# A convolution and a gated two-layer product on one core: a cast and a load moved in the opening, two PSUM banks and the last store changed at the end

## The chip, the cores and the metric

The kernel runs on one core of one Trainium2 chip. The metric is the device time of one execution in microseconds; the median of three runs is used. Five engines run their own queues in program order and wait for each other by semaphores: TensorE (PE, with its weight loads as PEld), VectorE (DVE), ScalarE (ACT), GpSimd (POOL) and SyncE (SP, which here issues nearly all DMAs). Matrix products land in PSUM[...].

## What is computed

```python
# x: (8, 4096, 192), weight: (8 heads, 7), w_in: (192, 2048), w_out: (2048, 192), all float32
w = softmax(weight, axis=-1)
# causal convolution over the sequence, each head of 24 channels with its own 7 weights
y[b, s, head] = sum_k w[head, k] * x[b, s - 6 + k, head]       # zeros ahead of the sequence
h = y.reshape(32768, 192) @ w_in
g = h * cos(h)
out = g @ w_out                                                # (32768, 192)
```

## The kernel before, in words

The 32768 tokens are cut into 32 units of 1024 and 64 tiles of 512. A unit is loaded (`load_unit`, L66), cast to bfloat16 with its channels reordered (`cast_unit`, L157: three copies, L170 for the even heads, L171 and L172 for the odd heads with the partition halves exchanged), convolved on PE with banded matrices (`conv_mm`, L177), copied out of PSUM (`conv_out`, L186), doubled on POOL (`double_unit`, L236) and transposed by a DMA (`turn_unit`, L240). A tile is then eight steps `h0` to `h7`: six matmuls each (`mm1`, L316) into one slot of a ring of three PSUM tiles of two banks (`h_pool`), the sine with a shift on ACT (L330), and the product on DVE (L334), which frees the slot. The product with w_out (`mm2_step`, L340) sums into two further banks, `o_ps0` and `o_ps1` (L347). It uses the upper and the lower 64 rows of the array at once, for different sums, so that two matmuls run side by side; since both row halves of a sum go to one bank, an SP instruction (`Turn`, L141) stands between the end of one half and the start of the other. `evac` (L359) copies a bank to SBUF on ACT, and `store` (L364) writes a tile of 384 KB.

The order on each engine is written out by hand: strings give PE's and ACT's order in a tile (L371 to L375), and the rest of the loop (L377 to L425) says where copies, transposes, loads and stores come in. Two extra rounds of that loop drain the pipeline: round 64 has only `mm2` work (the last tile's sums begin, those of the tile ahead end), round 65 only the last 32 matmuls, those of the last sum's second row half.

The opening, L61 to L310, is a chain of its own. SP loads unit 0 in halves, w_in in four parts and unit 1. PE computes matmuls on zeros (`keep_warm`, L93) while DVE makes the banded weights: a product of 2128 columns (L253) and four sums (L256) give `prod`, and eight small copies, dealt out to DVE, ACT and POOL (L259 to L264), put it into `band`; three casts of w_in follow (L266). The first half of unit 0 is cast by ACT, the second half by POOL, both ahead of the bands in program order (L249 and L250). PE convolves the first half (two groups of eight matmuls), the second (two groups), and then transposes the first half itself (`turn_first`, L282); ACT and DVE copy each group out. The second half goes through `double_unit` and `turn_unit` (L301 and L302), after which SP issues the four loads of w_out (L303 to L305), POOL casts the second half of w_in (L306), unit 1 (L307) and w_out in two halves (L308 and L309), and unit 2 is loaded (L310). The first tile runs with the convolution of unit 1 among its steps (L374).

Of the kernel before, what the change touches and what calls it, by code (L numbers as in the profile page):

```python
# [8 lines left out]
FP32 = mybir.dt.float32  # L9
# [7 lines left out]
def kernel(  # L17
# [8 lines left out]
    nc = tc.nc  # L26
# [5 lines left out]
    T = 512  # L32
    NT = NTOK // T
    NB = T // 128
    U = 1024
    NU = NTOK // U
    UB = U // 128
# [18 lines left out]
    o_pools = [ctx.enter_context(tc.tile_pool(name=n, bufs=1, space=PSUM)) for n in ("o_p", "o_q")]  # L56
# [20 lines left out]
    HP = NP // 2  # L77
    for q in range(2):
        for t in range(2):
            nc.sync.dma_start(out=w_f[64 * t : 64 * t + 64, :, q * HP : (q + 1) * HP, :].rearrange("p k j f -> p k (j f)"),  # L80
                              in_=w_src[t, :, :, q * HP * 128 : (q + 1) * HP * 128])
    load_unit(1)
    wo_f = consts.tile([128, NP, 2, D], FP32)
    wo_src = moe_w_out.rearrange("(i j p) d -> p j i d", i=2, p=128)


    one = consts.tile([128, 128], FP32)
    nc.vector.memset(one, 1.0)
# [4 lines left out]
    def keep_warm(n):  # L93
        for _ in range(n):
            nc.tensor.matmul(out=idle, lhsT=zero[:, 0:128], rhs=zero, start=True, stop=True)  # L95
# [4 lines left out]
    w_all = o_pools[1].tile([128, T], FP32, name="o_ps1")  # L100
    w_bc = w_all[:, 0 : H * K].rearrange("p (h k) -> p h k", k=K)
    nc.tensor.matmul(out=w_all[:, 0 : H * K], lhsT=one[0:1, :], rhs=w_row, start=True, stop=True)
    keep_warm(16)


    xb0 = xbf_pool.tile([128, UB + 1, D], BF16, name="x_bf")
# [50 lines left out]
    def cast_unit(u, n0=0, n1=UB):  # L157
        copy = nc.scalar.copy if u == 0 and n0 == 0 else nc.gpsimd.tensor_copy
        if u == 0:
            bf[u] = xb0  # L160
        else:
            bf[u] = xbf_pool.tile([128, UB + 1, D], BF16, name="x_bf")
            if u % UPS == 0:
                nc.gpsimd.memset(bf[u][:, 0, :], 0.0)
            else:
                nc.gpsimd.tensor_copy(out=bf[u][:, 0, :], in_=bf[u - 1][:, UB, :])  # L166

        o = bf[u][:, n0 + 1 : n1 + 1, :].rearrange("p n (h t k r) -> t p (n h) k r", t=2, k=NC, r=R)
        i = x_tiles[u][:, n0:n1, :].rearrange("p n (h t r k) -> t p (n h) k r", t=2, k=NC, r=R)
        copy(out=o[0], in_=i[0])  # L170
        copy(out=o[1, 0:64], in_=i[1, 64:128])  # L171
        copy(out=o[1, 64:128], in_=i[1, 0:64])  # L172
        bf.pop(u - 2, None)
# [23 lines left out]
    def ring_banks():  # L197
        h = h_pool.tile([128, 2, T], FP32, name="h")
        return [h[:, 0, :], h[:, 1, :]]
# [36 lines left out]
    def double_unit(u, n0=0, n1=UB):  # L236
        ct = ct_tiles[u]
        nc.gpsimd.tensor_copy(out=ct[:, n0:n1, :, 1, :], in_=ct[:, n0:n1, :, 0, :])  # L238

    def turn_unit(u, n0=0, n1=UB):  # L240
        ct = ct_tiles.pop(u)
        if u not in cT:
            cT[u] = cT_pool.tile([128, UB, NC, 128], BF16, name="cT")
        nc.sync.dma_start_transpose(out=cT[u][:, n0:n1].rearrange("p n c k -> p (n c) k"),
                                    in_=ct[:, n0:n1].rearrange("p n c t k -> p (n c t k)"))
        cT.pop(u - 2, None)


    cast_unit(0, 0, NB)  # L249
    cast_unit(0, NB, UB)  # L250

    prod = consts.tile([128, K, H, E], BF16)
    nc.vector.tensor_tensor(out=prod, in0=mask.rearrange("p k (o e) -> p k o e", o=1).to_broadcast([128, K, H, E]),  # L253
# [6 lines left out]
    for odd in range(2):  # L260
        for q in range(4):
            e0 = 32 * (q ^ (2 * odd))
            three[(4 * odd + q) % 3](out=band[32 * q : 32 * q + 32, odd:H:2, e0 : e0 + E],  # L263
                                     in_=prod[32 * q : 32 * q + 32, 0, odd:H:2, :])  # L264
    for k in range(NC):
        three[(k + 2) % 3](out=w[:, k, 0:HP], in_=w_f[:, k, 0:HP])  # L266

# [4 lines left out]
    def conv_first(n0, n1):  # L272
        for c in range(2):
            ps = ring_banks()
            for i in range(4):
                for prev in range(2):
                    conv_mm(0, c, ps, i, slice(0, 128), prev, n0, n1, start=prev == 0 and i % 2 == 0, stop=prev == 1)
            yield
            for half in range(2):
                conv_out(0, c, ps, n0, n0 + 2 * half, n0 + 2 * half + 2, copies[half], double=n0 == 0)  # L280
# [12 lines left out]
    b = conv_first(NB, UB)  # L293
# [6 lines left out]
        list(across[half])  # L300
    double_unit(0, NB, UB)  # L301
    turn_unit(0, NB, UB)  # L302
    for q in range(2):  # L303
        for i in range(2):
            nc.sync.dma_start(out=wo_f[:, q * HP : (q + 1) * HP, i], in_=wo_src[:, q * HP : (q + 1) * HP, i])  # L305
    nc.gpsimd.tensor_copy(out=w[:, :, HP:NP], in_=w_f[:, :, HP:NP])  # L306
    cast_unit(1)  # L307
    for q in range(2):  # L308
# [19 lines left out]
    def gcu(t, j, h):  # L328
        cs = cos_pool.tile([128, 2, T], BF16, name="cs")
        nc.scalar.activation(out=cs, in_=h, func=AF.Sin, bias=math.pi / 2.0, scale=1.0)  # L330
        if j == 0:
            g_tiles[t] = gpool.tile([128, NF, T], BF16, name="g")
            g_tiles.pop(t - 3, None)
        nc.vector.tensor_tensor(out=g_tiles[t][:, 2 * j : 2 * j + 2, :], in0=h, in1=cs, op=ALU.mult)  # L334
# [5 lines left out]
    def mm2_step(t, q):  # L340
        half, i = divmod(q, STEPS)
        f, si = divmod(i, 2)
        for r, (tt, b) in enumerate(((t - 1, half), (t - 1, 0) if half else (t - 2, 1))):
            if not 0 <= tt < NT:
                continue
            if r == 0 and i == 0:
                o_ps[tt, b] = o_pools[b].tile([128, T], FP32, name="o_ps%d" % b)  # L347
            rows = slice(64 * r, 64 * r + 64)
            s = 2 * b + si
            m = nc.tensor.matmul(out=o_ps[tt, b][:, si * D : (si + 1) * D],  # L350
                                 lhsT=g_tiles[tt][rows, f, s * 128 : (s + 1) * 128], rhs=wo[rows, f // 2, f % 2, :],
                                 start=(r == 0 and i == 0), stop=(r == 1 and i == STEPS - 1), skip_group_check=True)
            if r == 0 and i == STEPS - 1:
                turns[tt, b] = Turn()
                turns[tt, b].mark(m)
            if r == 1 and i == 0:
                turns.pop((tt, b)).wait(m)

    def evac(t, b):  # L359
        if b == 0:  # L360
            o_sb[t] = opool.tile([128, NB, D], FP32, name="o_sb")
        nc.scalar.copy(o_sb[t][:, 2 * b : 2 * b + 2, :].rearrange("p s d -> p (s d)"), o_ps.pop((t, b))[:, 0 : 2 * D])  # L362

    def store(t):  # L364
        nc.sync.dma_start(out=out[t * T : (t + 1) * T, :].rearrange("(n p) d -> p n d", p=128), in_=o_sb.pop(t))

    o_ps, o_sb, turns = {}, {}, {}

# [8 lines left out]
    for t in range(NT + 2):  # L377
        u, second = divmod(t, TPU)
        cu, cc = (u + 2, 0) if second else (u + 1, 1)
        conv = {"c": conv_part(cu, cc, ring_banks if t else o_banks) if cu < NU else iter(())}  # L380
        if t == 0:
            conv["d"] = conv_part(1, 0, o_banks)
        act, done, h, step = (ACT_ORDER if t > 1 else ACT_FIRST[t]).split(), set(), {}, 0

        def flush():
            while act:
                k = act[0]
                need = {"P": "start", "Q": "|", "e": k[1:] + "2"}.get(k[0], "h" + k[1:])
                if need not in done:
                    return  # L390
                act.pop(0)
                if k == "P" and 0 <= t - 2 < NT:
                    evac(t - 2, 0)
                elif k == "Q" and 0 <= t - 2 < NT:
                    evac(t - 2, 1)
                elif k[0] == "e":
                    next(conv[k[1]], None)
                elif k[0] == "s" and t < NT:
                    gcu(t, int(k[1:]), h.pop(int(k[1:])))

        done.add("start")
        flush()
        for k in (PE_ORDER if t > 1 else PE_FIRST[t]).split():
            if k[0] == "h" and t < NT:
                h[int(k[1:])] = mm1(t, int(k[1:]))
            elif k[0] in conv:
                next(conv[k[0]], None)
            elif k[0] == "m":
                for q in range(step, step + int(k[1:])):
                    mm2_step(t, q)  # L410
                step += int(k[1:])
            done.add(k)
            flush()

            if k == ("|" if t == 0 else "h1") and second == 0 and cu < NU:
                double_unit(cu)
            if k == "|":
                if second == 0 and cu < NU:
                    turn_unit(cu)
                if 0 <= t - 2 < NT:  # L420
                    store(t - 2)
                if second == 1 and u + 3 < NU:
                    load_unit(u + 3)
                if second == 0 and u + 2 < NU:
                    cast_unit(u + 2)  # L425
# [30 lines left out]
```

## Time and profile before

The time is 737.81 us, the median of three runs from 736.77 to 737.82. The profiled execution has a span of 736.2 us.

| | |
|---|---|
| one tile, at 100 to 111 us, all engines | 11.04 us; PE busy 11.04, DVE 9.52, ACT 9.67, POOL 2.62 |
| warm-keeping matmuls, first to last | 1.33 to 7.81 us |
| first matmul of the convolution | 10.85 us |
| first matmul of the first tile | 16.37 us |
| granted PE clock from 11.97 to 15.38 us | 0.50 of full |
| last matmul ends, last copy by ACT | 732.1 us, 732.15 to 732.63 us |
| w_out loads issued; landed | 17.4 to 19.1 us; 4.1, 4.7, 6.1 and 8.1 us later |
| last store issued; landed | 732.68 us; 2.5 us later |

In the lines of the timeline the first number is the start, the second the time from the start of the first to the end of the last instruction of the row, then the engine, the source line, the operation, what it writes and reads, how many instructions, and in brackets how long the engine had been idle and what ended that. "PEld" is a weight load, "SPq" an instruction of SP's queue. In the page's second part each digit is the busy tenth of a fortieth of the span.

### The profile page before, as it was taken

The page shows a single profiled execution, that of the slowest core. Times are in us where ns is not written, and L with a number is a line of the kernel's source. Part 1 is how long each engine was busy: PE and PEld are TensorE (multiplying, and loading weights), DVE is VectorE, ACT ScalarE, POOL GpSimd, SP SyncE. Part 2 cuts the span into 40 slices and gives each one's busy share as a digit, 9 for nine tenths or more (in the row PEclk, how much of TensorE's full clock was granted, in tenths as well). Part 3 has the DMA queues.
Part 4 walks back from the last instruction along what each step waited for, and adds up shares of the span by engine and source line. Part 5 has one row for each costly group of instructions (what it writes and reads, how often), then busy time and mean ns, then how long its engine had stood idle before and what let it go on. Part 6 is the DMA issues. An engine that isn't in the chain of part 4 may idle for free.

```text
span 736.2 us, 26768 instructions
## 1 busy us (share of the span) xinstructions
PE 720.7 (98%) x12073; PEld 554.7 (75%) x12073; DVE 621.1 (84%) x538; ACT 626.8 (85%) x785; POOL 179.2 (24%) x177
## 2 busy tenths in 40 slices
PE   6799999999999999999999999999999999999997
PEld 3577777777777777777777777777777777777776
DVE  6888888888888888888888888888888888888883
ACT  5888888888888888888888888888888888888883
POOL 6522211222211222211222211222211222211000
PEclk9999999999999999999999999999999999999999
DMA  7734334344345454334344334344335455333301
GB/s 190 199 86 131 86 111 129 87 111 130 81 116 131 86 111 130 88 110 130 87 110 130 89 110 130 87 110 130 89 108 132 87 110 125 94 108 87 89 23 66
DMA packets 167941, 79.97 MB, mean 109 GB/s; under 512 B 99475, under 2 KB 167059, under 8 KB 167827
## 3 DMA queue, kind: packets, MB, share of 16 engines
q1 hardware_dynamic: 167824, 78.26, 40.3%
q8 instruction: 94, 1.54, 0.9%
q14 instruction: 21, 0.16, 0.1%
q10 hardware_dynamic: 2, 0.00, 0.0%
HBM read 28.31 MB, written 25.17 MB: 73 GB/s over the span
## 4 chain that ended last, share of the span: by engine, by line
PE 95%; ACT 0%; issue 0%; SPq 0%
PE o_ps L350 46%; PE h L324 45%; PE h L180 4%; ACT o_sb L362 0%; SPq L146 0%
## 5 line engine op out<-in xcount | busy, mean ns | idle before, releaser
L334 DVE TENSOR_TENSOR g<-h,cs 128x1024 bf16<-128x1024 f32 x512 | 609.1, 1221 | 98.4 <-ACT cs L330 89.8
L330 ACT ACTIVATE cs<-h 128x1024 bf16<-128x1024 f32 x512 | 511.5, 1025 | 79.7 <-PE h L324 78.4
L350 PEld LDWEIGHTS <-g 64*128 64x128 bf16 x8192 | 362.2, 94 | 68.1 <-SPq L146 1.8
L350 PE MATMUL o_ps<-wo,g 64*128 64x192 bf16 x8192 | 409.1, 243 | 1.8 <-ACT o_sb L362 1.2
L324 PE MATMUL h<-cT,w 64*128 64x512 bf16 x3072 | 401.4, 376 | 2.6 <-DVE g L334 1.4
L324 PEld LDWEIGHTS <-w 64*128 64x128 bf16 x3072 | 166.4, 94 | 85.3 <-issue 3.6
L238 POOL COPY ct<-ct 128x1536 bf16<-128x1536 bf16 (+1 forms) x32 | 46.2, 1444 | 492.5 <-issue 489.3
L362 ACT COPY o_sb<-o_ps 128x384 f32<-128x384 f32 x128 | 61.3, 479 | 11.0 <-PE o_ps L350 8.2
L195 ACT CAST ct<-h 128x384 bf16<-128x384 f32 (+1 forms) x124 | 52.4, 474 | 9.8 <-PE h L180 5.9
L180 PE MATMUL h<-x_bf,band 64*128 64x192 bf16 (+1 forms) x752 | 54.3, 243 | 5.1 <-DVE band L263 3.0
L180 PEld LDWEIGHTS <-band 64*128 64x128 bf16 (+1 forms) x776 | 38.7, 95 | 18.9 <-POOL band L263 3.9
L170 POOL CAST x_bf<-x_f 128x768 bf16<-128x768 f32 (+1 forms) x32 | 40.4, 1262 | 2.0 <-DMA x_f<-in_x_dram 2.0
L171 POOL CAST x_bf<-x_f 64x768 bf16<-64x768 f32 (+1 forms) x32 | 38.9, 1216 | 2.0
L172 POOL CAST x_bf<-x_f 64x768 bf16<-64x768 f32 (+1 forms) x32 | 38.5, 1204 | 1.9
L166 POOL COPY x_bf<-x_bf 128x192 bf16<-128x192 bf16 x24 | 8.2, 343 | 0.0
L95 PE MATMUL o_ps<-zero 128*128 128x512 bf16 x19 | 6.0, 473 | 1.3 <-DVE zero L90 1.3
L95 PEld LDWEIGHTS <-zero 128*128 128x128 bf16 x19 | 2.0, 114 | 4.0 <-issue 1.4
L309 POOL CAST wo<-wo_f 128x1536 bf16<-128x1536 f32 x2 | 2.9, 1466 | 4.7 <-DMA wo_f<-in_moe_w_out_dram 4.7
L263 ACT COPY band<-prod 32x152 bf16<-32x152 bf16 x3 | 0.9, 316 | 2.6 <-DVE prod L256 2.6
L256 DVE TENSOR_TENSOR prod<-prod 128x304 bf16<-128x304 bf16 (+1 forms) x4 | 2.7, 705 | 0.1
L253 DVE TENSOR_TENSOR prod<-mask,wn 128x2128 bf16<-128x2128 bf16 x1 | 2.4, 2376 | 0.1
L180 PE MATMUL o_ps<-x_bf,band 64*128 64x192 bf16 x24 | 2.0, 242 | 0.5 <-ACT ct L195 0.3
(43 smaller groups left out, 28.0 us busy)
## 6 DMA issues: line engine op xcount, KB each, us to landing
out_dram<-o_sb SPq DMA_DIRECT2D x64, 384.0 KB, 2.9
x_f<-in_x_dram SPq DMA_DIRECT2D x31, 768.0 KB, 5.2
w_f<-in_moe_w_in_dram SPq DMA_DIRECT2D x4, 384.0 KB, 8.1
wo_f<-in_moe_w_out_dram SPq DMA_DIRECT2D x4, 384.0 KB, 5.4
x_f<-in_x_dram SPq DMA_DIRECT2D x2, 384.0 KB, 4.0
cT<-ct SPq DMA_TRANSPOSE x32, 4.6
w_row<-in_weight_dram ACTq DMA_DIRECT2D x1, 0.2 KB
```

Source lines behind the costliest of these rows:

```text
L166: nc.gpsimd.tensor_copy(out=bf[u][:, 0, :], in_=bf[u - 1][:, UB, :])
L170: copy(out=o[0], in_=i[0])
L171: copy(out=o[1, 0:64], in_=i[1, 64:128])
L172: copy(out=o[1, 64:128], in_=i[1, 0:64])
L180: return nc.tensor.matmul(out=ps[i // 2][:, 0 : (n1 - n0) * 2 * G].rearrange("p (n k i r) -> p i n k r", n=n1 - n0, k=NC, i=2)[:, i % 2], ...
L195: copy(o[:, :, 0, :], i[:, :, 0, :])
L238: nc.gpsimd.tensor_copy(out=ct[:, n0:n1, :, 1, :], in_=ct[:, n0:n1, :, 0, :])
L324: nc.tensor.matmul(out=h[:, i, :], lhsT=w[rows, k, j, :], rhs=c[rows, n0 : n0 + NB, k, :], start=(k == 0), stop=(k == NC - 1))
L330: nc.scalar.activation(out=cs, in_=h, func=AF.Sin, bias=math.pi / 2.0, scale=1.0)
L334: nc.vector.tensor_tensor(out=g_tiles[t][:, 2 * j : 2 * j + 2, :], in0=h, in1=cs, op=ALU.mult)
L350: m = nc.tensor.matmul(out=o_ps[tt, b][:, si * D : (si + 1) * D], lhsT=g_tiles[tt][rows, f, s * 128 : (s + 1) * 128], rhs=wo[rows, f // 2, ...
L362: nc.scalar.copy(o_sb[t][:, 2 * b : 2 * b + 2, :].rearrange("p s d -> p (s d)"), o_ps.pop((t, b))[:, 0 : 2 * D])
```

## The change

Four edits. In the opening, the second half of unit 0 is cast by POOL after the eight band copies instead of ahead of them, and PE computes 26 matmuls on zeros instead of 16 while it waits, so that POOL leaves DVE alone while the bands are made. Half of w_out is loaded right behind unit 1, ahead of the transpose of unit 0's second half, so that it is there when POOL comes to cast it. At the end, the last tile's two sums go into the two banks of a slot of the ring, which is free by then, instead of `o_ps0` and `o_ps1`, so that they need not wait for the evacuation of the tile ahead; and the last tile is stored in two halves, each when its bank has been copied. The changed kernel's lines are 4 to 11 higher than those of before: the sums are L261, the band copies L268, the cast L176 to L178, the w_in casts L272, `mm1` L328, the sine L334, the product L338, `mm2` L358, `evac` L370, `store` L373.

```diff
+    def load_wo(q):
+        for i in range(2):
+            nc.sync.dma_start(out=wo_f[:, q * HP : (q + 1) * HP, i], in_=wo_src[:, q * HP : (q + 1) * HP, i])
+
+    load_wo(0)
...
-    keep_warm(16)
+    keep_warm(26)
...
     cast_unit(0, 0, NB)
-    cast_unit(0, NB, UB)
...
             three[(4 * odd + q) % 3](out=band[32 * q : 32 * q + 32, odd:H:2, e0 : e0 + E],
                                      in_=prod[32 * q : 32 * q + 32, 0, odd:H:2, :])
+    cast_unit(0, NB, UB)
...
     turn_unit(0, NB, UB)
-    for q in range(2):
-        for i in range(2):
-            nc.sync.dma_start(out=wo_f[:, q * HP : (q + 1) * HP, i], in_=wo_src[:, q * HP : (q + 1) * HP, i])
+    load_wo(1)
...
             if r == 0 and i == 0:
-                o_ps[tt, b] = o_pools[b].tile([128, T], FP32, name="o_ps%d" % b)
+                if tt < NT - 1:
+                    o_ps[tt, b] = o_pools[b].tile([128, T], FP32, name="o_ps%d" % b)
+                elif b == 0:
+
+                    o_ps[tt, 0], o_ps[tt, 1] = ring_banks()
...
-    def store(t):
-        nc.sync.dma_start(out=out[t * T : (t + 1) * T, :].rearrange("(n p) d -> p n d", p=128), in_=o_sb.pop(t))
+    def store(t, b0=0, b1=2):
+        nc.sync.dma_start(out=out[t * T + b0 * 256 : t * T + b1 * 256, :].rearrange("(n p) d -> p n d", p=128),
+                          in_=o_sb[t][:, 2 * b0 : 2 * b1, :])
...
                     evac(t - 2, 0)
+                    if t == NT + 1:
+                        store(t - 2, 0, 1)
...
-                    store(t - 2)
+                    store(t - 2, 1 if t == NT + 1 else 0)
```

## The prediction

> **What bounds the kernel now.** I read the page first, then the chain of waits, then the opening and the end in the timeline. The page says that TensorE is the bound, and where it is not:
>
> ```profile
> span 736.2 us, 26768 instructions
> ...
> PE 720.7 (98%) x12073; PEld 554.7 (75%) x12073; DVE 621.1 (84%) x538; ACT 626.8 (85%) x785; POOL 179.2 (24%) x177
> ...
> PE   6799999999999999999999999999999999999997
> ...
> PE 95%; ACT 0%; issue 0%; SPq 0%
> ```
>
> Only the first two slices and the last of PE are under 9. In the chain of waits cut to the first 45 us, PE follows PE without a break from 34.25 us on ("34.25 0.04 issue" is its first piece), so any shift of that point moves all that follows, up to 721 us. The tiles between repeat every 11.04 us and the change does not touch them. So the time is: when PE becomes gapless, plus a fixed middle, plus the tail. The opening:
>
> ```profile
> 5.73 2.22 POOL L170 CAST x_bf<-x_f 128x384 bf16<-128x384 f32 x1 [2.00 <-DMA x_f<-in_x_dram]
> ...
> 7.43 2.81 DVE L256 TENSOR_TENSOR prod<-prod 128x912 bf16<-128x912 bf16 x4
> ...
> 8.01 0.98 POOL L171 CAST x_bf<-x_f 64x384 bf16<-64x384 f32 x1
> ...
> 9.04 0.68 POOL L172 CAST x_bf<-x_f 64x384 bf16<-64x384 f32 x1
> ...
> 10.82 0.13 PEld L180 LDWEIGHTS <-band 128*128 128x128 bf16 x2 [3.50 <-POOL band L263]
> ...
> 15.27 0.96 DVE L290 CAST cT<-h 128x768 bf16<-128x768 f32 x1 [0.45 <-PE h L286]
> ...
> 16.37 2.12 PE L324 MATMUL h<-cT,w 64*128 64x512 bf16 x18 [1.14 <-DVE cT L290]
> ...
> 27.36 1.47 POOL L309 CAST wo<-wo_f 128x1536 bf16<-128x1536 f32 x1 [3.14 <-DMA wo_f<-in_moe_w_out_dram]
> ...
> 28.77 1.47 POOL L238 COPY ct<-ct 128x1536 bf16<-128x1536 bf16 x1
> ...
> 33.02 0.32 PE L180 MATMUL h<-x_bf,band 64*128 64x192 bf16 x3 [0.49 <-POOL x_bf L171]
> ...
> 34.29 0.24 PE L180 MATMUL h<-x_bf,band 64*128 64x192 bf16 x1 [0.94 <-POOL x_bf L172]
> ```
>
> POOL's cast of unit 0's second half and DVE's sums (L256) run side by side and slow each other. PE waits for the bands until 10.82, starts the tiles at 16.37, and at 33 to 34 us waits twice for POOL, which is late because it stood 3.14 us before the second w_out cast. The windows by stage show the granted clock of PE at 1.00 up to 11.97, 0.50 from there to 15.38, then 1.00. The end:
>
> ```profile
> 722.48 0.48 ACT L362 COPY o_sb<-o_ps 128x384 f32<-128x384 f32 x1
> ...
> 723.01 2.82 PE L350 MATMUL o_ps<-wo,g 64*128 64x192 bf16 x64 [0.58 <-ACT o_sb L362]
> ...
> 726.41 5.70 PE L350 MATMUL o_ps<-wo,g 64*128 64x192 bf16 x96 [0.58 <-ACT o_sb L362]
> ...
> 732.15 0.48 ACT L362 COPY o_sb<-o_ps 128x384 f32<-128x384 f32 x1 [2.39 <-PE o_ps L350]
> ```
>
> PE stops twice for an evacuation, but not a third time (the x96 is 64 and 32 with 0.04 between).
>
> **What the Trainium skill says.** "SBUF — State Buffer", Who interferes with whom: a VectorE operation with two SBUF inputs, or in a two-port mode, and a GpSimd operation that reads SBUF exclude each other for a whole instruction. The trace agrees: POOL's 384-column cast took 2.22 us while DVE's L253 held on until 7.40, and DVE's equal 304-column sums took 0.69 and 0.70 beside POOL but 0.32 alone. "TensorE: Matmul & The Clock Gate", Part 1: an idle window of about 3.4 us halves the clock, a busy one restores it. The trace agrees: PE stood from 7.81 to 10.85, and the half clock lasted 3.41 us. "PSUM — Partial Sum Buffer", PSUM bank collisions raise a hardware error: two engines on one bank must be kept apart. The trace shows DVE's L193 starting only after ACT's. "DMA: Bandwidth & Descriptors", Anatomy of one DMA: about 2 us fixed, the rest by bytes. The last store landed 2.5 us after issue, with traffic for only 1.15 of them.
>
> **Part 1, second half of the cast behind the bands, 26 warm-keepers for 16.** The four sums: the last, alone, took 0.32; after a block ended, the 912-column one needed 0.49 and a 304-column one 0.18, so 608 columns cost 0.31 and the first alone is 0.63. Sum 0.63 + 3 x 0.32 + 3 gaps of 0.03 = 1.68 instead of 2.81: the bands start at 9.11 + 0.04 instead of 10.28, 1.13 earlier. The warm-keepers cost 0.213 us each at full clock, so ten more end at 7.81 + 2.13 = 9.94; the odd heads' bands come at 10.23 (11.36 - 1.13), so these ten cost nothing while the clock is up, and they take away the idle window, so I take full clock for the opening's matmuls. What is added: on POOL the three casts now stand behind two band copies (end 9.88) and ahead of the w cast, which only the tile at 15.0 needs. Alone each is some 0.63 (half of the 1.23 of 768 columns); DVE's w cast, which took 0.87 beside POOL, gets in once for some 0.28. They end at 9.92 + 3 x 0.65 + 0.28 = 12.1 (11.8 to 12.5). PE's third group of eight waits for that; ahead of it 16 matmuls are done by 10.8. Behind it stand the fourth group and the 12 transposing matmuls. So PE: third group to 12.4, fourth to 12.75 (8 x 0.04), transposes to 13.45 (12 x 0.057). ACT's outputs of groups 3 and 4 run 12.6 to 13.36; DVE follows ACT, 13.47 to 13.88, then its cT copy of 0.96 to 14.87. The first tile starts at 15.0 instead of 16.37: 1.37 gained (0.6 to 1.8). The w_in half for the casts landed at 9.85 (2.45 + 7.4 to landing) and is just in time.
>
> **Part 2, half of w_out early.** Two loads (0.79 MB) enter SP's queue behind unit 1, at 5.04. Transfers ran at some 225 GB/s until 15.1 and the engines then stood to 17; the loads fill that gap and end near 18, so the transpose, issued near 14.5, moves its data after them, done near 19.5; its half is needed at 24. Unit 1 landed at 15.84 and POOL wants it at 16.5: hidden, with little to spare. The second half of w_out then lands near 22.3 instead of 27.2. POOL: unit 1 cast 16.2 to 20.25, w_out 20.3 to 21.75 and 22.4 to 23.9, so it is free when ACT's last convolution output of tile 0 comes (27.39 - 1.37 = 26.0). The doubling copy starts at 26.1 instead of 28.77, and the cast of unit 2 ends at 31.6 instead of 34.23. PE reaches the convolution at 32.23 - 1.37 = 30.86 and its last matmul waits till 31.6. Then the next h needs the buffer that DVE's fourth product frees, 33.30 - 1.37 + 0.1 = 32.05. So PE becomes gapless at 32.1 where it was 34.29: 2.2 gained in the opening (1.2 to 2.8), of which 0.8 belong to part 2.
>
> **Part 3, ring banks at the end.** Both stops of 0.58 go: starts were 3.40 apart (723.01 to 726.41) and 2.89 where no evacuation was awaited, so each was worth 0.51. But both banks of the last tile are one tile, and in the built program the first of the last 32 matmuls waits for ACT's copy of the other half. Behind that wait stand only those 32, and ACT's last copy and the last store wait for them. So a stop of 0.51 is added: 2 x 0.51 - 0.51 = 0.51 gained. The ring slot was freed by DVE's product at about 721.4, before 722.4: no wait.
>
> **Part 4, store by halves.** The first half leaves under the last matmuls. The last store has half the bytes: 1.15 us of traffic becomes 0.58, landing 1.9 instead of 2.5: 0.57 gained (0.2, if fixed costs rule, to 0.7). The end gives 1.1.
>
> **Rivals.** (a) POOL is the new bound, or the clock falls again (PE is busy only 38% of 11.6 to 15.0): the third group comes at 12.5 and the matmuls after it cost double (20 x 0.05 = 1.0). Then the opening gives 1.0, all 735.7. For: DVE and POOL share what both need just then. Against: even late, 12.5 is near the old 12.0. (b) The end gives only the shorter store, because the handover through SP takes the place of ACT's wait (it was 0.30 at 729.29), and the added stop costs its 0.51: 735.5. (c) Slower: the early w_out halves share the engines with w_in and unit 1 rather than queue behind them. For: unit 2's load and w_out overlapped, landing at 29.2 and 27.2. Unit 1 then lands at 18.5, POOL's cast ends at 22.4 instead of 20.3 (2.1 lost), w_in is 1.5 late with ACT's and DVE's outputs queued behind it, and the first products fall into a half-clock window (1.5). Opening 2.2 - 5.1 = -2.9, end +1.1: 739.6. Against: within one queue the first loads landed in the order of issue (4.2, 5.6, 7.6, 9.85 us). (d) Better: the cast ends at 11.7 (0.4 more), DVE lets go of the ring 0.4 sooner, and ACT's stop in the opening shrinks with it, 3.2 in the opening and 1.3 at the end: 733.3.
>
> **Numbers.** 737.81 - 2.2 - 1.1 = 734.5. Forecast 0.60, (a) 0.14, (b) 0.10, (c) 0.06, (d) 0.10. Faster by over 0.2% (under 736.3) holds in the forecast, in (d) and in most of (a) and (b): 0.84; no change 0.11, slower 0.05. Range 733.0 to 736.3: it leaves out (c) and the tails of (a) and (d).
>
> **What would show it.** Sums L261 at 1.7 us; bands from 9.1; POOL's casts of the second half ending near 12.1; granted clock 1.00 at 12 to 15; first tile matmul near 15.0; no w_out wait above 1 us on POOL; PE gapless from 32.1; no stop before the two last 64s, one of about 0.5 before the last 32; the last store near 1.9. Wrong if unit 1's cast waits for its load, or the first tile starts after 16.

## The result and the profile after

The changed kernel takes 734.81 us, the median of four runs from 734.79 to 734.92. That is 0.9963 of the time before (95% interval 0.9946 to 0.998): 3.0 us less by the medians, 1.5 to 4.0 us by the interval. The kernel before was run beside every experiment below: its medians there lay between 737.50 and 737.77 and its single times between 736.2 and 738.1. That spread of almost 2 us turned out to be part of the answer. The changed kernel itself has only these four runs.

The page after, in the same lines as before:

```profile
span 733.1 us, 26791 instructions
...
PE 723.0 (99%) x12083; PEld 554.6 (76%) x12083; DVE 620.0 (85%) x538; ACT 626.9 (86%) x785; POOL 177.5 (24%) x177
...
PE   7899999999999999999999999999999999999997
...
PE 98%; DVE 1%; ACT 1%; issue 0%
```

The span is 3.1 us shorter and the middle is the same: the last 24 matmuls of round 63 start at 721.26 us before and 719.27 after, 1.99 earlier, and from there to the end it is 14.94 and 13.83. So in these two profiles 1.99 us came from the opening and 1.11 from the end. The timeline of the opening after (start, length of the row, engine, line, operation; in brackets the idle time and what ended it):

```profile
7.14 0.15 PEld L101 LDWEIGHTS <-zero 128*128 128x128 bf16 x1 [0.28 <-issue]
7.43 1.57 DVE L261 TENSOR_TENSOR prod<-prod 128x912 bf16<-128x912 bf16 x4
...
11.00 0.93 PE L186 MATMUL h<-x_bf,band 128*128 128x96 bf16 x18
11.46 0.70 POOL L178 CAST x_bf<-x_f 64x384 bf16<-64x384 f32 x1
...
12.21 0.42 PE L186 MATMUL h<-x_bf,band 128*128 128x96 bf16 x6 [0.28 <-POOL x_bf L178]
...
15.38 2.12 PE L328 MATMUL h<-cT,w 64*128 64x512 bf16 x18 [1.14 <-DVE cT L296]
...
22.99 1.47 POOL L313 CAST wo<-wo_f 128x1536 bf16<-128x1536 f32 x1 [0.83 <-DMA wo_f<-in_moe_w_out_dram]
...
26.46 1.47 POOL L244 COPY ct<-ct 128x1536 bf16<-128x1536 bf16 x1 [2.00 <-ACT ct L201]
27.35 4.96 DVE L338 TENSOR_TENSOR g<-h,cs 128x1024 bf16<-128x1024 f32 x4 [0.46 <-ACT cs L334]
...
31.98 0.24 PE L186 MATMUL h<-x_bf,band 64*128 64x192 bf16 x1 [0.27 <-POOL x_bf L178]
...
32.36 0.82 PE L328 MATMUL h<-cT,w 64*128 64x512 bf16 x6
```

DVE's sums take 1.57 us instead of 2.81, and POOL's cast ends at 12.16. But the warm-keepers are still spaced at 0.43 us until 7.55, half speed, so they end near 11.1 and the convolution starts at 11.00, not at the 9.6 at which its bands allow it. The first tile starts at 15.38 instead of 16.37. The chain of waits up to there runs through the keepers, and POOL's cast is not in it:

```profile
3.39 7.77 PE o_ps L101 x26
11.16 0.35 PE h L186 x8
11.54 0.55 ACT ct L199 x2
...
12.88 0.52 PE h L186 x8
13.41 0.84 PE h L292 x12
14.28 0.97 DVE cT L296
...
15.38 0.84 PE h L328 x6
```

The third group of matmuls waits 0.28 us for POOL, but the fourth, at 12.88, waits for DVE's copy of the first group, whose slot of the ring it takes; that copy is late because the convolution starts late.

On POOL the wait for w_out shrinks from 3.14 to 0.83, the doubling copy starts at 26.46 instead of 28.77 and now waits for ACT, and PE becomes gapless at 32.36 instead of 34.29, 0.05 after DVE's four products end (27.35 + 4.96 = 32.31). The chain of waits at the end:

```profile
723.35 2.82 PE h L358 x63
726.17 0.02 issue
726.19 0.49 ACT o_sb L370
726.68 0.04 issue
726.72 2.81 PE h L358 x32
729.53 0.02 issue
729.55 0.48 ACT o_sb L370
```

`h` is here the slot of the ring that holds both sums, one in each of its two banks (a bank is here 512 float32 columns of a PSUM tile). The two stops of before are gone and the one ahead of the last 32 matmuls is there: 726.17 to 726.72. The last store lands 1.9 us after its issue.

### The profile page after: what moved, and what is told of

Read it like the earlier page. It is cut to its first block, busy times and chain, and to the rows that moved or that the text cites. A ratio compares the mean times of both kernels' runs of the same rounds, so it can differ in the third digit from the quotient of the medians.

```text
span 733.1 us, 26791 instructions
## 1 busy us (share of the span) xinstructions
PE 723.0 (99%) x12083; PEld 554.6 (76%) x12083; DVE 620.0 (85%) x538; ACT 626.9 (86%) x785; POOL 177.5 (24%) x177
## 4 chain that ended last, share of the span: by engine, by line
PE 98%; DVE 1%; ACT 1%; issue 0%
PE o_ps L358 46%; PE h L328 45%; PE h L186 4%; PE o_ps L101 1%; PE h L358 1%; DVE g L338 1%; ACT cs L334 0%; ACT ct L201 0%; PE o_ps L186 0%; DVE cT L296 0%; ACT o_sb L370 0%; PE h L292 0%; PE o_ps L108 0%; ACT ct L199 0%; DVE ct L199 0%
## 5 line engine op out<-in xcount | busy, mean ns | idle before, releaser
L338 DVE TENSOR_TENSOR g<-h,cs 128x1024 bf16<-128x1024 f32 x512 | 609.1, 1221 | 97.4 <-ACT cs L334 88.8
L334 ACT ACTIVATE cs<-h 128x1024 bf16<-128x1024 f32 x512 | 511.5, 1025 | 78.4 <-PE h L328 77.1
L358 PEld LDWEIGHTS <-g 64*128 64x128 bf16 x8192 | 362.0, 94 | 67.8 <-issue 1.2
L328 PE MATMUL h<-cT,w 64*128 64x512 bf16 x3072 | 401.3, 376 | 2.7 <-DVE g L338 1.4
L358 PE MATMUL o_ps<-wo,g 64*128 64x192 bf16 x8064 | 403.3, 243 | 0.6 <-ACT ct L201 0.6
L328 PEld LDWEIGHTS <-w 64*128 64x128 bf16 x3072 | 166.1, 94 | 84.9 <-issue 3.0
L370 ACT COPY o_sb<-o_ps 128x384 f32<-128x384 f32 x126 | 60.4, 479 | 5.1 <-PE o_ps L358 2.4
L186 PEld LDWEIGHTS <-band 64*128 64x128 bf16 (+1 forms) x776 | 38.2, 94 | 14.9 <-issue 1.3
L178 POOL CAST x_bf<-x_f 64x768 bf16<-64x768 f32 (+1 forms) x32 | 38.6, 1206 | 1.9
L176 POOL CAST x_bf<-x_f 128x768 bf16<-128x768 f32 (+1 forms) x32 | 38.8, 1213 | 0.1
L101 PE MATMUL o_ps<-zero 128*128 128x512 bf16 x29 | 9.3, 489 | 1.3 <-DVE zero L96 1.3
L358 PE MATMUL h<-wo,g 64*128 64x192 bf16 x128 | 8.7, 243 | 0.6 <-ACT o_sb L370 0.6
L370 ACT COPY o_sb<-h 128x384 f32<-128x384 f32 x2 | 1.0, 480 | 5.2 <-PE h L358 5.2
```

The costliest lines, as they stand in the source:

```text
L186: return nc.tensor.matmul(out=ps[i // 2][:, 0 : (n1 - n0) * 2 * G].rearrange("p (n k i r) -> p i n k r", n=n1 - n0, k=NC, i=2)[:, i % 2], ...
L328: nc.tensor.matmul(out=h[:, i, :], lhsT=w[rows, k, j, :], rhs=c[rows, n0 : n0 + NB, k, :], start=(k == 0), stop=(k == NC - 1))
```

## The experiments

All kernels are the changed one with the edit shown, except `before26`, which is the kernel before with one edit. Times are in microseconds; "more" is the median against 734.81, the median of the four runs of the changed kernel.

| run | edit | runs | median | lowest to highest | more |
|---|---|---|---|---|---|
| `cast_ahead` | cast ahead of the bands | 8 | 735.21 | 735.18 to 736.01 | 0.40 |
| `keep16` | 16 warm-keepers | 17 | 735.66 | 734.76 to 736.43 | 0.85 |
| `keep21` | 21 warm-keepers | 7 | 735.64 | 734.77 to 736.41 | 0.83 |
| `wo_late` | no early w_out | 6 | 735.35 | 734.75 to 735.59 | 0.54 |
| `cast_and_wo` | cast ahead and no early w_out | 9 | 735.37 | 735.20 to 736.00 | 0.56 |
| `ring_off` | last sums in o_ps0, o_ps1 | 10 | 735.51 | 735.38 to 736.24 | 0.70 |
| `store_whole` | one last store | 11 | 735.62 | 735.21 to 737.34 | 0.81 |
| `before26` | before, 26 keepers | 13 | 736.78 | 736.27 to 737.12 | 1.97 |
| `two_slots` | last sums in two slots | 5 | 734.26 | 734.24 to 734.58 | -0.55 |
| `act_cast21` | ACT casts the even heads, 21 keepers | 5 | 734.47 | 734.04 to 735.87 | -0.34 |
| `best26` | ACT casts, two slots, 26 keepers | 5 | 733.73 | 733.53 to 734.30 | -1.08 |
| `best_gaps` | as that, 21 keepers, six in gaps | 5 | 733.90 | 733.53 to 734.78 | -0.91 |

**The cast order alone.**

```diff
     cast_unit(0, 0, NB)
+    cast_unit(0, NB, UB)
...
-    cast_unit(0, NB, UB)
     for k in range(NC):
```

> The changed kernel with the second half of unit 0 cast ahead of the bands again, and the 26 warm-keepers kept. Theory 1 (the forecast: the bands come 1.1 us sooner and that is what shortens the opening): the sums take 2.8 us again, the first tile starts near 16.1 to 16.4 and the kernel takes 735.5 to 735.8. Theory 2 (the bands' lead is eaten, since the keepers end at 11.2 in the profile after and the third group then waits for POOL until 12.2; the full clock is what shortens the opening): the first tile starts near 15.6, at most 0.25 us later than with the cast behind the bands, and the kernel takes 734.8 to 735.0.

Six of eight runs lie at 735.2: 0.40 more, between the two theories and nearer to the second. The profile is of one of the other two runs (735.93, with a half clock from 16 to 19.4 us, after the first tile has started). In it the bands come 1.3 us later (10.32 for 9.03), the convolution starts at 10.89 with two matmuls and goes on at 11.40, instead of 11.00, and the first tile starts at 15.70 instead of 15.38. So of the 1.3 us by which the new order brings the bands sooner, 0.3 to 0.4 arrive.

**The warm-keepers alone.**

```diff
-    keep_warm(26)
+    keep_warm(16)
```

> The changed kernel with 16 warm-keepers, all else as changed. Theory 1 (keepers hold the clock): PE stands some 1.5 to 2 us before the convolution, the granted clock falls to a half somewhere between 12 and 15.4 us, the third and fourth group and the transposes take about twice as long, the first tile starts near 16.0 and the kernel takes 735.2 to 735.5. Rival (the ten keepers only delay the convolution): the clock stays full, the convolution starts near 10.2, the first tile near 15.0, and the kernel takes 734.4 to 734.6.

Both happened, each in some of the runs, and both ranges were missed. Eight of seventeen runs lie at 734.76 to 734.89, as with 26, and not at 734.4 to 734.6; nine lie at 735.66 to 736.43, above the 735.2 to 735.5 of theory 1. The profile is one of the second kind. Its timeline of PE, and the window from 15 to 18 us (busy time and number of PE, PEld, DVE, ACT, POOL, then granted clock, DMA share, GB/s):

```profile
10.11 0.84 PE L186 MATMUL h<-x_bf,band 128*128 128x96 bf16 x16 [0.23 <-ACT band L268]
12.17 1.28 PE L186 MATMUL h<-x_bf,band 128*128 128x96 bf16 x14 [1.22 <-POOL x_bf L178]
13.25 1.48 PE L292 MATMUL h<-ident,ct 128*128 128x128 bf16 x12
15.87 1.47 PE L328 MATMUL h<-cT,w 64*128 64x512 bf16 x6 [1.14 <-DVE cT L296]
```

```profile
15.00:18.00 3.00, 2.13 (x12) 0.91 (x14) 0.72 (x1) 0.63 (x1) 3.00 (x4) 0.50 1.15 296
```

PE stood from 7.66 to 9.64, the granted clock fell to 0.50 at 11.6 and stayed there until 21.9, and the transposes took 1.48 us as before instead of 0.83. So the ten keepers save nothing at best and 0.9 to 1.6 us otherwise. What they change is how often that happens. The nine runs have a mean granted clock over the whole run of 0.991 to 0.996, the eight 0.998 or more. With 26 keepers and the same opening (the changed kernel and `ring_off`, `two_slots` and `store_whole` below), six of thirty runs have 0.996 and none less: in these runs 26 make the half clock rarer, but they do not rule it out.

```diff
-    keep_warm(26)
+    keep_warm(21)
```

> The changed kernel with 21 warm-keepers. Theory (beyond the time the bands come, keepers only delay; and the third group waits for POOL until 12.2 all the same): the convolution starts near 10.1 instead of 11.0, ACT's and DVE's outputs of the first two groups come 0.9 sooner, the fourth group follows the third, and the first tile starts near 15.1 instead of 15.38: 734.5 to 734.6 while the clock stays full, and few or no runs with a half clock. Rival (26 are needed to hold the clock): a second group of times at 735.6 or more, as with 16.

The rival holds: three runs lie at 734.8 and four at 735.64 or more. The theory also fails in its good case, since 734.8 is no better than with 26. In the profile, of a run at 736.01, the convolution starts at 9.63 and the third group still waits for POOL until 12.17.

**w_out behind the transpose.**

```diff
-    load_wo(0)
...
     turn_unit(0, NB, UB)
+    load_wo(0)
     load_wo(1)
```

> The changed kernel with both halves of w_out loaded behind the transpose, as before. Theory (the early half frees POOL for the doubling copy): POOL waits about 3 us for the second half, doubles unit 1 near 27.7 instead of 26.5, PE waits for the last cast of unit 2 until some 33.2, and PE becomes gapless near 33.3 instead of 32.36: 735.6 to 735.8. Rival (the load was hidden anyway, DVE's ring sets the point): 734.8, no change.

The median is 0.54 more, where 0.8 to 1.0 was expected; two of the six runs, at 734.75 and 734.80, show no loss at all. The timeline of a run with the loss:

```profile
25.85 1.47 POOL L312 CAST wo<-wo_f 128x1536 bf16<-128x1536 f32 x1 [1.10 <-DMA wo_f<-in_moe_w_out_dram]
...
32.79 0.24 PE L184 MATMUL h<-x_bf,band 64*128 64x192 bf16 x1 [0.93 <-POOL x_bf L176]
32.80 0.88 PE L327 MATMUL h<-cT,w 64*128 64x512 bf16 x6
```

The mechanism is the forecast's: POOL waits 2.82 and 1.10 us for the two halves, and PE waits 0.93 for POOL's last cast and is gapless at 32.80. But the second half landed before 25.85, not at the 27.2 of the kernel before, so less was at stake.

**Cast and w_out together.**

```diff
-    load_wo(0)
...
     cast_unit(0, 0, NB)
+    cast_unit(0, NB, UB)
...
-    cast_unit(0, NB, UB)
     for k in range(NC):
...
     turn_unit(0, NB, UB)
+    load_wo(0)
     load_wo(1)
```

> The changed kernel with both the cast ahead of the bands and both halves of w_out behind the transpose, as before; 26 warm-keepers and the new end stay. Undone alone the first cost 0.40 us and the second 0.54, together they stand for 0.94. Theory 1 (they add up, since the first moves the first tile and the second POOL's wait in the tile): 735.7 to 735.8. Theory 2 (a later first tile hides the wait for w_out, since the loads are issued from SP at nearly the same time): about 735.2, no more than the cast alone. The kernel before with 26 keepers, whose lowest time is 736.27, speaks for the second: with 1.1 less at the end it would be 735.2.

The result is nearer to the second theory: 735.37, and four of nine runs at 735.20 to 735.22, the lowest times of `cast_ahead`. The two parts overlap: behind the later first tile, the loss of the early w_out is 0.16 by the medians and nothing by the lowest times. In the profile (735.22) the first tile starts at 15.68, the waits for w_out on POOL are 2.16 and 0.87 us, and PE is gapless at 32.66.

**The last tile's banks.**

```diff
-                if tt < NT - 1:
-                    o_ps[tt, b] = o_pools[b].tile([128, T], FP32, name="o_ps%d" % b)
-                elif b == 0:
-
-                    o_ps[tt, 0], o_ps[tt, 1] = ring_banks()
+                o_ps[tt, b] = o_pools[b].tile([128, T], FP32, name="o_ps%d" % b)
```

> The changed kernel with the last tile's sums in o_ps0 and o_ps1 again, the store still in halves. Theory: two stops of 0.5 us come back and the one before the last 32 matmuls goes, 0.5 to 0.6 us longer: 735.3 to 735.45. Rival (the handover through SP would take the place of ACT's wait): 734.8.

The median is 0.70 more, the lowest time 0.59. Within the profiles, from the start of the last 24 matmuls in the chain of waits to ACT's last copy it is 10.71 us (719.53 to 730.24) against 10.10 (719.45 to 729.55): 0.61.

```diff
-                elif b == 0:
-
-                    o_ps[tt, 0], o_ps[tt, 1] = ring_banks()
+                else:
+                    o_ps[tt, b] = ring_banks()[0]
```

> The changed kernel with the last tile's two sums in the first banks of two ring slots, so that the last 32 matmuls do not wait for ACT's copy of the other sum. Theory: the stop of 0.57 us ahead of the last 32 goes, the handover through SP leaves 0.05: 0.5 us less, 734.3. Rival (the handover takes its place): 734.8.

As the theory said: 734.26. The chain of waits has no stop for ACT between the last two stretches of matmuls any more:

```profile
723.20 2.81 PE h L357 x63
726.01 0.02 issue
726.03 2.82 PE h L357 x32
```

The handover through SP costs 0.02 us here. So the third stop came from putting both sums into one tile, and the change could have had about 1.1 us from its banks (0.61 and 0.55 together), not 0.6.

**The store in one piece.**

```diff
-                    if t == NT + 1:
-                        store(t - 2, 0, 1)
...
-                    store(t - 2, 1 if t == NT + 1 else 0)
+                    store(t - 2)
```

> The changed kernel with the last tile stored in one piece of 384 KB after both copies. Theory (half the bytes, the fixed part stays): the last store lands 2.5 us after its issue instead of 1.9, 0.5 to 0.6 us longer: 735.3 to 735.4. Rival (the fixed part rules): 734.9 to 735.0.

The last store lands 2.5 us after its issue instead of 1.9, and the lowest time is 735.21, 0.42 above the lowest with halves. The median is 0.81 more, but that is not the store alone: five of the eleven runs have a mean granted clock of 0.996 instead of 0.998 or 0.999 and take 736.05 or more. The profiled one, 736.07, is among them, with a clock of 0.50 from 14.9 to 18.4 us, long before the store. Its last store gives a cleaner figure: from the end of ACT's last copy to the end of the span it is 3.6 us against 3.1, so half the bytes gain 0.4 to 0.5. If the time to land is a straight line through the two sizes, about 1.3 us of it do not depend on the size; that is an estimate from 2.5 us for 384 KB and 1.9 for 192 KB.

**Keepers in the kernel before.**

```diff
-    keep_warm(16)
+    keep_warm(26)
```

> The kernel before with 26 warm-keepers for 16 and nothing else. Theory (what keepers buy is that the clock is not halved in the opening, where the kernel before nearly always is): most runs at 736.2 to 736.6, some 1 us under the median of before, with less spread. Rival (the cast order is what the opening gains from, keepers only delay): 737.6 or more.

The median is 736.78 against 737.77 beside it, with runs from 736.27 to 737.12. Ten matmuls on zeros and nothing else give 1.0 us by the medians, a third of the whole change; the ratio, 0.999 (0.9981 to 0.9998), gives 0.7 us (0.1 to 1.4). The lowest time does not move (736.23 for the kernel before in all its runs): here too the keepers change how often the half clock comes, not the best time. The first tile starts here:

```profile
15.68 1.16 PE L324 MATMUL h<-cT,w 64*128 64x512 bf16 x6 [1.14 <-DVE cT L290]
```

That is 0.69 earlier than before with the bands where they were (10.30 for 10.28): the clock is at 1.00 from 8 to 16 us, and the half clock comes from 16.0 to 19.4, after the first tile has started. Some of the thirteen runs have a mean clock of 1.000 and so no such stretch; none of these was profiled.

**A lighter POOL, and a better kernel.** ACT stands idle from 7.7 to 9.0 us, so it can take a third of POOL's cast.

`cast_unit` gets a further argument: 2 casts the even heads alone, by ACT, and 1 the odd heads, by POOL.

```diff
-    keep_warm(26)
+    keep_warm(21)
...
     cast_unit(0, 0, NB)
+    cast_unit(0, NB, UB, 2)
...
-    cast_unit(0, NB, UB)
+    cast_unit(0, NB, UB, 1)
```

> 21 warm-keepers, and the even heads of unit 0's second half cast by ACT ahead of the bands, where it stands idle from 7.7 to 9.0 us; POOL keeps the two odd-head casts behind the bands. Theory (POOL's three casts set the third group): POOL ends near 11.3 instead of 12.2, all four groups run on from 10.1, and the first tile starts 0.3 to 0.9 us sooner than with 21 keepers alone: 733.8 to 734.2. Rival (the copies by ACT and then DVE set it): no difference to 21 keepers alone.

The median is 734.47 and the lowest 734.04, against 735.64 and 734.77 with 21 keepers alone. That is the direction of the theory, and the spread of almost 2 us is again that of 21 keepers.

```profile
11.44 0.42 PE L188 MATMUL h<-x_bf,band 128*128 128x96 bf16 x6 [0.49 <-POOL x_bf L180]
...
14.71 2.12 PE L331 MATMUL h<-cT,w 64*128 64x512 bf16 x18 [1.14 <-DVE cT L299]
```

The third group starts 0.77 us sooner than in the profile after (11.44 for 12.21), and the first tile 0.67 sooner (14.71 for 15.38). Part of that is the smaller number of keepers. Against `two_slots`, where the keepers also end early and the third group waits for POOL, the first tile is 0.53 sooner (14.71 for 15.24), which is nearer to what the lighter POOL is worth alone.

> The changed kernel with the last tile's sums in two ring slots, and the even heads of unit 0's second half cast by ACT ahead of the bands; 26 warm-keepers. Theory: the end gives 0.5 as in the run with two slots alone; the opening gives 0.7 where the keepers run at full clock from 5 us and end near 10, and next to nothing where they end near 11.1, so two groups of times, 733.5 and 734.2, and none above 734.6. Rival: a half clock in some runs all the same, 735.3.

It takes both edits, the ring slots as in `two_slots` and the cast as in `act_cast21`, and is faster than either: 733.73, 0.9951 of the time before (0.9939 to 0.9964), with no run above 734.3. In its profile, of the run at 734.30, the keepers end near 11.07 and the first tile still starts at 15.30, so there the opening's part is small, as expected.

```diff
-    keep_warm(26)
+    keep_warm(21)
...
     list(conv_first(0, NB))
+    keep_warm(2)
...
     for half in range(2):
         list(across[half])
+    keep_warm(4)
```

> As the last, but with 21 warm-keepers ahead of the bands, two more between the second and the third group of the convolution and four behind the transposes, where PE stands. Theory (a half clock comes from stretches in which PE is idle, wherever they lie, so keepers in the gaps do what those ahead of the bands do): the times fall at 733.5 to 733.7 and few at 735. Rival (keepers ahead of the bands are what counts): two groups as with 21 keepers alone, the upper one at 735.0 to 735.5.

The median is 733.90, with four of five runs from 733.53 to 733.90 and one at 734.78. That one is 1.25 us above the lowest, as far as the upper group of 21 keepers alone, but its mean granted clock is 1.000, where that group has 0.991 to 0.996. So none of the five shows a half clock, and what held the one up is open. With five runs it is not shown that this is better or worse than 26 keepers ahead of the bands.

## Why the prediction was right, and where it was not

The time, 734.5 for 734.81, and its split, 2.2 and 1.1 for 1.99 and 1.11, came out. The steps inside did less well, and the opening's 2.2 is right only against the usual run of the kernel before. In their lowest times the two kernels are 1.4 us apart (736.23, the lowest of 80, and 734.79), and 1.1 of that is the end; where the kernel before keeps its clock, the new opening gains some 0.3 us, by an estimate from these times.

- **Sums and bands.** Right: 1.57 for 1.68 us, bands at 9.03 for 9.15. POOL's cast ends at 12.16 for 12.1.
- **"These ten cost nothing while the clock is up."** This failed as a premise. In the profile after, the keepers ran at half speed until 7.55 and ended near 11.1, not at 9.94, and held the convolution until 11.00. In all profiles together the full spacing began between 4.6 and 7.6 us, though the first of these matmuls starts at 1.33 in each. The Trainium skill, "TensorE: Matmul & The Clock Gate", Part 1 (The HAM clock gate), says that the window of the clock gate is free-running, so that the same kernel sees different numbers of slow matmuls; these starts agree with it, but the page gives ±0.5 us as the spread, and here it is 3.0 us.
- **The idle window.** The prediction took PE's stand of 3.04 us for the window that halves the clock. The 3.41 us ahead of the half clock hold that stand and 0.85 us of work, so, if the window ends where the clock falls, it need not be empty; in `store_whole` there were 1.89 us of work in the 3.41 us ahead of the fall. So keepers ahead of the bands are no guarantee: with 26 of them, six of thirty runs still had the lower clock.
- **The bands' lead carried to the first tile, 1.37.** Mis-sized, and put down to the wrong part. The profiles give 0.99. Of that, 0.69 is the clock alone (`before26`), and the cast order is worth about 0.3 more (15.70 to 15.38). The rest of the bands' lead is lost in either case. If the keepers end late, they hold the convolution: so it is in the chain of waits after, and with POOL relieved but the keepers late, in `best26`, the first tile still starts at 15.30. If they end early, the third group waits for POOL until 12.2 (`keep16`, `keep21`, `two_slots`): in the chain of waits of `two_slots` stand POOL's three casts, from 9.86 to 12.13, and the first tile starts at 15.24. `act_cast21`, with a lighter POOL and early keepers, gains 0.53 over that.
- **w_out early, 0.8.** Right in its chain, too large: 0.54 when it alone is undone, and 0.16 by the medians where the first tile is late. DVE's ring as the next bound was right: 32.36 for 32.1.
- **Ring banks, 0.51; halves, 0.57.** Right in mechanism and close in size: 0.61 in the profiles (0.70 by the medians) for the banks, 0.4 to 0.5 for the halves. The stop that the shared tile adds measured 0.55, and taking it away gave 0.55 in the time.
- **The rivals.** (a), POOL as the new bound or the clock falling again, is what some runs do: where the keepers end early POOL is the bound, and in `store_whole` the clock falls too; in the profile after neither holds. (b) is excluded by `ring_off`, which loses 0.61 us when the banks are undone, and by `two_slots`, where the handover costs 0.02 us. (c) did not happen: POOL's cast of unit 1 starts at 16.87 with no wait for its load.

What stays open is what sets the phase of the clock gate from run to run, and so which of its times a run takes. It was seen, not controlled. The profiles are one run each, and the share of runs with a half clock rests on the mean clocks of runs that were not profiled.

## What to carry to other kernels

Cost an opening with more than one phase of the clock: a move that saves work on one engine may gain or lose by where PE's idle time falls, and cheap matmuls on zeros in that idle time bought here a third of the gain by the medians and fewer runs with a half clock, but no better lowest time. When a producer is sped up, look at what stands next in the consumer's queue: the bands came 1.25 us sooner, but the same keepers that held the clock held PE until 11.0, and where they ended early POOL's displaced cast held the third group of matmuls until 12.2. When two results share one tile, look at what the program makes each wait for: here one stop of 0.55 us, gone with a second tile.

## What the runs showed of the hardware that was not expected

- The granted clock in the windows is 1.00 from the start in all profiles, but the matmuls of 512 columns stood 0.43 us apart at first and 0.21 later. The half speed of the start is seen in the spacing only.
- In `keep16` the half clock lasted from 11.6 to 21.9 us, three times the 3.41 us of the kernel before. In the first two of these three stretches PE was busy for 2.56 and 2.59 us of 3.41, in the third for all of it. In the kernel before it was busy for 2.91 of 3.41, and the full clock came back at once. Where the limit lies these runs do not show.
- The two early w_out loads kept SP issuing for 3.43 us (from 5.15), where the first two took some 1.2 us in the kernel before (from 17.37). The loads ahead of them were still on their way in the first case. No one waited for SP then: its next DMA, the transpose, is issued at 15.24.
